# Counting tiny weights on GpSimd behind the channel layers, in place of zeroing them while they are rounded

## The chip, the core and the metric

The kernel runs on one core of one Trainium2 chip. The core has five engines that run side by side and wait for each other through semaphores: PE (TensorE: matrix products, with its weight loads PEld beside them), DVE (VectorE), ACT (ScalarE), POOL (GpSimd) and SP (SyncE, which here issues all DMAs, one after the other). The metric is the device time of one launch in microseconds (us). Before the change it is 819.13 us, the median of three runs (819.13 to 821.41).

## The reference, cut to what matters

```
attention: B,H,S,D = 4,8,768,48            # f = sigmoid(f_logit)
  state = f[t] * state + k[t] v[t]^T ;  y[t] = q[t] state      # a gated linear recurrence
spatial MLP on x = y (768 x 384 per batch):
  h = relu(x @ w_in);  u, v = halves of h;  v_n = layernorm(v)
  v_s = w_spatial @ v_n + b_spatial;  x = (u * v_s) @ w_out
mixer:
  u = x + (relu(x^T @ w_tok1) @ w_tok2)^T                       # token layer
  out = u + relu(u @ w_ch1) @ w_ch2                             # channel layer, width 1536
```

The weights w_in, w_out, w_tok1, w_tok2, w_ch1 and w_ch2 arrive as 64-bit floats, w_spatial and the activations as 32-bit ones. Results are 32-bit.

## The kernel before, in words

One program handles the four batches in turn. Every matrix product that needs full precision is done as three passes: each operand is split into a high and a low part (h and l), and PE computes h*h, h*l and l*h (`mm3`, lines 158 to 164).

The first stage (about 0 to 445 us) goes through the batches. For each batch it does the attention (`att`, 8 units of two heads and half a sequence; a unit starts with the load `fkq` of 578 KB), then the spatial MLP (`s1` gives the halves u and v, `s23` mixes over the sequence and multiplies by w_out, result `x1d` in DRAM). Units of the next batch's attention are woven between the matrix products of the present one. The second stage (about 445 us to the end) does the token layer (`c1`, `c2`) and the channel layer (`ff`): for each batch and each half of the sequence, 12 steps, each with 9 matmuls up (`up1`), a relu on ACT (`hh`, line 641), its low part on DVE (`hl`, line 642) and 9 matmuls down (`down`, line 654).

Before a 64-bit weight can be used it is turned into 32 bits by integer operations, in pieces of 128 x 384 (47 of them). That is the function `rounded` (lines 58 to 80): SP loads the raw words (`st`), DVE shifts and joins the high word (lines 66 and 69), ACT scales the low word (line 73), POOL adds it with rounding (line 74), ACT squares the high word, read as a 32-bit float (line 75), and DVE multiplies the result by "square >= bound" (line 79). A double too small for a normal 32-bit float so becomes zero. w_in and w_out are used at once (`split_weight`). The other four are rounded early, stored to DRAM (`round_weight`, store on line 93) and read back as 32-bit numbers later. Pools limit how many pieces are under way: three buffers for `st`, three for the result.

A second body, written for general inputs (`body(True)`), stands behind a branch and runs only if `flag` is set; the flag comes from the smallest gate product (`pend`, lines 550 to 556) and is read by all engines at the end (line 710). It does not run with these inputs.

The functions emit instructions in program order, in lists that `weave` mixes. A scheduler then orders each engine's instructions by its own estimate of when they are ready, and picks a free buffer for each tile. So the order on each engine and on SP's queue is fixed before the run: whatever stands first and waits holds up all that stands behind it.

Of the kernel before, what the change touches and what calls it, by code (L numbers as in the profile page):

```python
# [8 lines left out]
F32 = mybir.dt.float32  # L9
# [9 lines left out]
def tile_kernel(ctx, tc, fkqs, v, w_in, w_sp, b_sp, w_out, w_t1, w_t2, w_c1, w_c2, out):  # L19
    nc = tc.nc  # L20
# [22 lines left out]
    def f32(ap):  # L43
        return ap.bitcast(F32)
# [8 lines left out]
    pend = const.tile([P, B * NP, NCH], F32, name="pend")  # L53


    LEAST = 3.4332275390625e-05 ** 2

    def rounded(stage, a, src, c0, width, name):

        st = stage.tile([P, WST, 2], U32, tag="wst", name=f"{name}st")  # L60
        nc.sync.dma_start(
            out=st[:, :width, :].rearrange("p c t -> p (c t)"), in_=src[:, 2 * c0 : 2 * (c0 + width)]
        )
        yield
        lo, hi = st[:, :width, 0], st[:, :width, 1]
        nc.vector.tensor_scalar(
            out=a, in0=hi, scalar1=3, scalar2=0x3FFFFFFF, op0=ALU.logical_shift_left, op1=ALU.bitwise_and
        )
        nc.vector.scalar_tensor_tensor(
            out=a, in0=hi, scalar=0xC0000000, in1=a, op0=ALU.bitwise_and, op1=ALU.bitwise_or  # L70
        )

        nc.scalar.activation(lo, lo, AF.Copy, scale=2.0**-29)
        nc.gpsimd.tensor_tensor(out=a, in0=a, in1=lo, op=ALU.add)
        nc.scalar.activation(f32(hi), f32(hi), AF.Square)
        yield

        a = f32(a)
        nc.vector.scalar_tensor_tensor(out=a, in0=f32(hi), scalar=LEAST, in1=a, op0=ALU.is_ge, op1=ALU.mult)
        return a  # L80

    def round_weight(stage, src, name):

        if src.dtype != mybir.dt.uint64:
            return src, []
        rows, cols = src.shape
        dst = dram.tile([rows, cols], F32, name=name + "d")
        srcr = src.bitcast(U32).rearrange("(n p) c -> n p c", p=P)

        def piece(i, c0, width):  # L90
            at = stage.tile([P, WST], U32, tag="wsa", name=f"{name}da{i}{c0}")
            a = yield from rounded(stage, at[:, :width], srcr[i], c0, width, f"{name}d{i}{c0}")
            nc.sync.dma_start(out=dst[i * P : (i + 1) * P, c0 : c0 + width], in_=a)

        return dst, [
            partial(piece, i, c0, min(WST, cols - c0)) for i in range(rows // P) for c0 in range(0, cols, WST)
        ]

    kept = {}

    def split_weight(pool, stage, src, name, n, cols, eng, first=0, order=None, psum=None):

        wide = src.dtype == mybir.dt.uint64
        h = pool.tile([P, n, cols], F32R, name=name + "h")
        l = pool.tile([P, n, cols], F32R, name=name + "l")
        if wide:
            src = src.bitcast(U32)
        srcr = src.rearrange("(n p) c -> n p c", p=P)

        def piece(i, c0, width):  # L110
            sl = (slice(None), i, slice(c0, c0 + width))
            at = stage.tile([P, WST], U32, tag="wsa", name=f"{name}sa{i}{c0}")
            a = at[:, :width]
            if wide:
                a = yield from rounded(stage, a, srcr[first + i], c0, width, f"{name}{i}{c0}")
                nc.scalar.copy(h[sl], a)
                yield
            else:
                a = f32(a)
                nc.sync.dma_start(out=a, in_=srcr[first + i][:, c0 : c0 + width])  # L120
                yield
                nc.scalar.copy(h[sl], a)
                yield
                yield
            if eng is not nc.tensor:
                eng.tensor_tensor(out=l[sl], in0=a, in1=f32(h[sl]), op=ALU.subtract)
                return

            ps = psum.tile([P, W], F32, tag="m", name=f"{name}pl{i}{c0}")[:, :width]
            nc.tensor.matmul(ps, ident, a, start=True, stop=False)  # L130
            nc.tensor.matmul(ps, minus, h[sl], start=False, stop=True)
            yield
            nc.scalar.copy(l[sl], ps)

        where = [(i, c0, min(WST, cols - c0)) for i in range(n) for c0 in range(0, cols, WST)]
        return h, l, [partial(piece, *x) for x in (order(where) if order else where)]
# [13 lines left out]
    def weave(main, *fillers):  # L150

        for n, m in enumerate(main):
            for fl in fillers:
                for x in fl[len(fl) * n // len(main) : len(fl) * (n + 1) // len(main)]:
                    x()
            m()
# [9 lines left out]
    def body(general):  # L166
# [289 lines left out]
        def s23(b):  # L456
# [39 lines left out]


        winh, winl, steps = split_weight(
            wr, wst, w_in, "win", NK, DFF, nc.tensor, order=lambda x: sorted(x, key=lambda y: -y[1]), psum=ps_m
        )  # L500
        weave(att(half(0, 0)), staged(steps))
        bb = const.tile([P, S], F32, tag="bb", name="bb")
        nc.sync.dma_start(out=bb, in_=b_sp.unsqueeze(0).to_broadcast([P, S]))
        wsph, wspl, st_a = split_weight(wl, wst, w_sp, "wsp", NCH, S, nc.tensor, psum=ps_m)
        wouth, woutl, st_b = split_weight(wl, wst, w_out, "wout", NJ, DM, nc.tensor, psum=ps_m)
        s10, a01, sa = s1(0, 0), att(half(0, 1)), staged(st_a)
        weave(a01[:8], sa[:6])
        weave(s10, a01[8:], sa[6:])
        out_steps = staged(st_b)
        rest = []  # L510
        early = []
        if not general:
            for name, src in (("wt1", w_t1), ("wt2", w_t2), ("wc1", w_c1), ("wc2", w_c2)):
                kept[name], x = round_weight(wst, src, name)
                early += x
            early = staged(early)
        part = lambda n: early[len(early) * n // 5 : len(early) * (n + 1) // 5]
        for b in range(B - 1):
            if b:
                weave(s1(b, 0), rest)  # L520
            a, rest = s1(b, 1), []
            m, rest = s23(b)
            steps = att(half(b + 1, 0) + half(b + 1, 1))
            cut = len(steps) * len(a) // len(a + m)
            weave(a, steps[:cut], out_steps if b == 0 else part(2 * b - 1))
            weave(m, steps[cut:], part(2 * b))
        right.close()
        wr2 = ExitStack()
        w2p = wr2.enter_context(tc.tile_pool(name="w2p", bufs=1, side="right"))
# [1 line left out]
        t2h, t2l, st_b = split_weight(w2p, wst, kept["wt2"], "wt2", NT1, S, nc.gpsimd)  # L531
        c1h, c1l, st_c = split_weight(w2p, wst, kept["wc1"], "wc1", NK - 1, DC, nc.gpsimd)
        c1w = [(c1h[:, c, :], c1l[:, c, :]) for c in range(NK - 1)]
        weave(rest + s1(B - 1, 0) + s1(B - 1, 1), staged(st_a + st_b))
        conv = st_c
        mid.close()
        w2q = wr2.enter_context(tc.tile_pool(name="w2q", bufs=1, side="right"))
# [7 lines left out]
        xhp = wr2.enter_context(tc.tile_pool(name="xhp", bufs=1, side="right"))  # L545
        h1p = wr2.enter_context(tc.tile_pool(name="h1p", bufs=1, side="right"))

        if not general:

            nc.vector.tensor_reduce(  # L550
                out=least, in_=pend.rearrange("p u c -> p (u c)"), op=ALU.min, axis=mybir.AxisListType.X
            )
            row = ps_s.tile([P, W], F32, tag="s", name="row")[:1, :P]
            nc.tensor.transpose(row, least, ident)
            nc.vector.tensor_reduce(out=least[:1], in_=row, op=ALU.min, axis=mybir.AxisListType.X)
            nc.vector.tensor_scalar(out=flag, in0=least[:1], scalar1=LOW, scalar2=None, op0=ALU.is_lt)


        st2 = {}

        def c1(b):
            d = st2[b] = {}
# [66 lines left out]
        def ff(b, hf):  # L629
# [4 lines left out]
            def up1(ft):  # L634
                uh, ul = st2[b]["u"]
                fsl = slice(ft * P, (ft + 1) * P)
                ps = ps_m.tile([P, W], F32, tag="m", name=f"p3{b}{hf}{ft}")
                mm3(ps, [(c1w[c][0][:, fsl], c1w[c][1][:, fsl], uh[:, c, tsl], ul[:, c, tsl]) for c in range(NK)])
                hh = h3p.tile([P, W], F32R, tag="hh", name=f"hh{b}{hf}{ft}")
                hl = h3p.tile([P, W], F32R, tag="hl", name=f"hl{b}{hf}{ft}")  # L640
                nc.scalar.activation(hh, ps, AF.Relu)  # L641
                nc.vector.scalar_tensor_tensor(  # L642
                    out=hl, in0=ps, scalar=0.0, in1=f32(hh), op0=ALU.max, op1=ALU.subtract
                )
                hs[ft] = hh, hl
# [14 lines left out]
            def step(n):  # L660
                if n in range(3, 3 + NK):
                    uh, ul = st2[b]["u"]
                    c = n - 3
                    us[c] = op.tile([P, W], F32, tag=f"us{c}", name=f"us{b}{hf}{c}")
                    nc.gpsimd.tensor_tensor(  # L665
                        out=us[c], in0=f32(uh[:, c, tsl]), in1=f32(ul[:, c, tsl]), op=ALU.add
                    )
                if n < NF:
                    up1(n)
                if n:  # L670
                    down(n - 1)
                if n == NF:
                    for c in range(NK):
                        ot = otp.tile([P, W], F32, tag="ot", name=f"ot{b}{hf}{c}")
                        nc.vector.tensor_tensor(out=ot, in0=po[c], in1=us[c], op=ALU.add)
                        nc.sync.dma_start(out=out[b, c * P : (c + 1) * P, tsl], in_=ot)
# [84 lines left out]
```

## Time and profile before

| what | before |
|---|---|
| median of three runs | 819.13 us |
| the profiled execution | 819.0 us |
| its span, first to last instruction | 817.2 us |
| granted TensorE clock, mean | 0.978 |
| busy: PE, PEld | 777.3 us (95%), 716.3 us (88%) |
| busy: DVE, ACT, POOL | 420.3 (51%), 289.1 (35%), 211.1 us (26%) |
| instructions | 12758 |
| read from HBM, written | 54.72 MB, 15.73 MB |

The busy shares are means over two unlike stages. In the page's 40 slices of about 20 us DVE stands at 6 to 9 tenths up to the 14th slice and at 1 to 3 tenths from the 24th; POOL falls to 0 for most of the last 16 slices, while PE is at 9 tenths in all but the last of them. What a change is worth has therefore to be read from the stage in which its instructions run.

### The profile page before, as it was taken

The numbers are of one execution on the slowest core, as the hardware profiler recorded it, in microseconds if no ns is written. First come the engines' busy times: TensorE is split into PE (matmuls) and PEld (weight loads), VectorE is DVE, ScalarE is ACT, GpSimd is POOL, SyncE is SP. The second block draws the span as 40 slices with busy tenths as digits, with TensorE's granted clock in tenths as the row PEclk, the third lists the DMA queues.
The fourth block names the chain that finished last, engine by engine and source line by source line (L and its number), as shares of the span: only waits on it lengthen the run. The fifth ranks groups of instructions, "written<-read, shape, count | busy, mean of one in ns | idle before, by whom it ended". The sixth has DMA issues, their size and how long they took to land.

```text
span 817.2 us, 12758 instructions
## 1 busy us (share of the span) xinstructions
PE 777.3 (95%) x4860; PEld 716.3 (88%) x4860; DVE 420.3 (51%) x820; ACT 289.1 (35%) x649; POOL 211.1 (26%) x265
## 2 busy tenths in 40 slices
PE   5899899898989999999999999999999999999996
PEld 3577688688779888899899999999999999999995
DVE  6968599899898846673552532122122212221211
ACT  5766464555553444231632531122111211221110
POOL 4524344555641212110760330004000400010000
PEclk9899899999999999999999999999999999999998
DMA  7563435766474321220441410002000200000000
GB/s 254 176 207 104 147 96 164 236 225 214 146 237 140 101 96 59 65 67 24 128 126 40 138 56 30 1 4 85 1 30 0 87 1 30 1 8 24 30 1 33
DMA packets 39847, 73.74 MB, mean 90 GB/s; under 512 B 5216, under 2 KB 29664, under 8 KB 39776
## 3 DMA queue, kind: packets, MB, share of 16 engines
q1 hardware_dynamic: 39776, 72.83, 27.7%
q8 instruction: 40, 0.66, 0.3%
q14 instruction: 31, 0.25, 0.1%
HBM read 54.72 MB, written 15.73 MB: 86 GB/s over the span
## 4 chain that ended last, share of the span: by engine, by line
PE 71%; DVE 10%; DMA 10%; issue 4%; ACT 2%; SPq 1%; POOL 1%; DVEq 0%; ACTq 0%; POOLq 0%
PE po L654 19%; PE p L164 8%; PE p L162 8%; PE p L163 8%; DMA fkq<-in_fkq 3%; PE ps L162 3%; PE ps L164 3%; PE ps L163 3%; PE pa L259 2%; PE py L309 2%; PE py L315 2%; PE px L162 2%; PE px L163 1%; PE px L164 1%; DVE pg L236 1%
## 5 line engine op out<-in xcount | busy, mean ns | idle before, releaser
L642 DVE SCALAR_TENSOR_TENSOR hl<-p,hh 128x384 fp32r<-128x384 f32 x96 | 53.3, 557 | 188.4 <-ACT hh L641 188.4
L641 ACT ACTIVATE hh<-p 128x384 fp32r<-128x384 f32 x96 | 47.2, 492 | 198.0 <-PE p L164 198.0
L654 PE MATMUL po<-hl,wc2h 128*128 128x384 f32 x288 | 97.3, 338 | 0.0
L654 PE MATMUL po<-hh,wc2l 128*128 128x384 f32 x288 | 96.7, 336 | 0.0
L665 POOL TENSOR_TENSOR us<-uh,ul 128x384 f32<-128x384 f32 x24 | 24.3, 1024 | 232.0 <-DVE ul L625 214.7
L654 PE MATMUL po<-hh,wc2h 128*128 128x384 f32 x288 | 75.0, 336 | 0.0
L162 PE MATMUL ps<-wsph,vh 128*128 128x384 f32 x192 | 67.5, 351 | 0.0
L163 PE MATMUL ps<-wspl,vh 128*128 128x384 f32 x192 | 66.4, 346 | 0.0
L164 PE MATMUL ps<-wsph,vl 128*128 128x384 f32 x192 | 66.1, 346 | 0.0
L164 PE MATMUL p<-uh,wc1l 128*128 128x384 f32 x192 | 65.0, 338 | 0.0
L264 POOL TENSOR_SCALAR_AFFINE_SELECT am<-am 128x384 f32<-128x384 f32 x64 | 46.9, 748 | 69.7 <-ACT am L263 69.5
L163 PE MATMUL p<-ul,wc1h 128*128 128x384 f32 x192 | 64.7, 337 | 0.0
L162 PE MATMUL p<-uh,wc1h 128*128 128x384 f32 x192 | 64.2, 338 | 0.0
L654 PEld LDWEIGHTS po<-hl,wc2h 128*128 128x128 f32 x288 | 54.1, 188 | 0.1
L654 PEld LDWEIGHTS po<-hh,wc2l 128*128 128x128 f32 x288 | 54.1, 188 | 0.0
L654 PEld LDWEIGHTS po<-hh,wc2h 128*128 128x128 f32 x288 | 52.3, 188 | 0.0
L236 DVE TENSOR_TENSOR_SCAN pg<-fs,first 128x384 f32<-128x384 f32 x32 | 33.3, 1039 | 22.2 <-ACT first L379 22.1
L259 PE MATMUL pa<-fkq 48*128 48x128 f32 x384 | 40.6, 316 | 3.0 <-ACT am L263 3.0
L259 PEld LDWEIGHTS pa<-fkq 48*128 48x128 f32 x384 | 30.5, 204 | 12.3 <-issue 4.3
L162 PEld LDWEIGHTS ps<-wsph,vh 128*128 128x128 f32 x192 | 37.1, 193 | 2.4 <-issue 1.6
L625 DVE TENSOR_TENSOR ul<-p,uh 128x384 fp32r<-128x384 f32 x24 | 13.4, 557 | 47.6 <-ACT uh L624 47.6
L163 PEld LDWEIGHTS ps<-wspl,vh 128*128 128x128 f32 x192 | 37.0, 193 | 0.5 <-issue 0.2
(419 smaller groups left out, 1928.5 us busy)
## 6 DMA issues: line engine op xcount, KB each, us to landing
fkq<-in_fkq SPq DMA_DIRECT2D x31, 578.0 KB, 4.5
vt<-in_v SPq DMA_DIRECT2D x8, 576.0 KB, 5.9
x1d<-xs SPq DMA_DIRECT2D x24, 192.0 KB, 2.0
xf<-x1d SPq DMA_DIRECT2D x12, 384.0 KB, 4.5
out<-ot SPq DMA_DIRECT2D x24, 192.0 KB, 2.0
wspsa<-in_w_sp SPq DMA_DIRECT2D x12, 192.0 KB, 2.6
wc1d<-wc1da SPq DMA_DIRECT2D x12, 192.0 KB, 2.4
wc2d<-wc2da SPq DMA_DIRECT2D x12, 192.0 KB, 2.2
```

What stands on the lines that cost most here:

```text
L162: nc.tensor.matmul(ps, lh, rh, start=first and i == 0, stop=False, **kw)
L163: nc.tensor.matmul(ps, lh, rl, start=False, stop=False, **kw)
L164: nc.tensor.matmul(ps, ll, rh, start=False, stop=i == n - 1, **kw)
L236: nc.vector.tensor_tensor_scan(out=pc, data0=fs[:, :W], data1=first, initial=0.0, op0=ALU.mult, op1=ALU.add)
L259: nc.tensor.matmul(pa[j][:, c, :], ki[64 * j : 64 * j + D, sl], qi[64 * j : 64 * j + D, sl], start=True, stop=True)
L264: nc.gpsimd.affine_select(out=am[j], in_=am[j], compare_op=ALU.is_ge, fill=0.0, base=0, pattern=[[0, NCW], [1, C]], channel_multiplier=-1,)
L309: nc.tensor.matmul(py[:112, c, :], now[c][:112, :112], qi[:112, c * C : (c + 1) * C], start=c == 0, stop=False, skip_group_check=True,)
L315: nc.tensor.matmul(py[64 * j : 64 * j + m, c, :], vt[:, c, h0 + D * j : h0 + D * j + m], am[j][:, c, :], start=False, stop=True, skip_grou ...
L641: nc.scalar.activation(hh, ps, AF.Relu)
L642: nc.vector.scalar_tensor_tensor(out=hl, in0=ps, scalar=0.0, in1=f32(hh), op0=ALU.max, op1=ALU.subtract)
L654: nc.tensor.matmul(po[c], l[:, ft, csl], r, start=ft == 0 and x == 0, stop=ft == NF - 1 and x == 2)
L665: nc.gpsimd.tensor_tensor(out=us[c], in0=f32(uh[:, c, tsl]), in1=f32(ul[:, c, tsl]), op=ALU.add)
```

## The change

Three things change.

1. In the first body `rounded` no longer squares (ACT) and no longer compares and multiplies (DVE). The general body, which needs the zeroing, keeps both, and now rounds the four later weights itself.
2. Instead the first body counts: 88 times a block of 192 columns of a raw 64-bit weight is loaded again (`look`), in the channel layer, one block per step of `ff`. POOL squares the high words, compares with a slightly larger bound, and adds the result to a tile `lows`. The blocks' buffers are taken from the rotation (tag) of the channel layer's low parts `hl`, which has 7 buffers instead of 4. In the last half, at its eighth step, `judge` reduces `lows` and `pend` to one flag: if any weight was tiny, the general body runs. It stood ahead of the channel layer before, without `lows`.
3. The pieces of the four later weights are dealt out in program order from the second batch on, over seven lists instead of five, the last of them in the fourth batch.

```
-        nc.scalar.activation(f32(hi), f32(hi), AF.Square)
+        if tiny:
+            nc.scalar.activation(f32(hi), f32(hi), AF.Square)
         yield
         a = f32(a)
-        nc.vector.scalar_tensor_tensor(out=a, in0=f32(hi), scalar=LEAST, in1=a, op0=ALU.is_ge, op1=ALU.mult)
+        if tiny:
+            nc.vector.scalar_tensor_tensor(
+                out=a, in0=f32(hi), scalar=LEAST**2, in1=a, op0=ALU.is_ge, op1=ALU.mult
+            )
         return a
...
+    NEED = 192
+    lows = const.tile([P, NEED], F32, name="lows")
...
+    def look(pool, src, n):
+
+        rows, cols = src.shape[1] , src.shape[2]
+        st = pool.tile([P, 2 * NEED], U32, tag="hl", bufs=7, name=f"look{n}")[:, : rows * cols]
+        nc.sync.dma_start(out=st.rearrange("p (n c) -> p n c", n=rows), in_=src)
+        to = lows[:, : rows * cols // 2]
+        hi = f32(st[:, 1::2])
+        nc.gpsimd.tensor_tensor(out=hi, in0=hi, in1=hi, op=ALU.mult)
+        nc.gpsimd.tensor_scalar(out=hi, in0=hi, scalar1=NEAR**2, scalar2=None, op0=ALU.is_lt)
+        nc.gpsimd.tensor_tensor(out=to, in0=to, in1=hi, op=ALU.add)
...
-        part = lambda n: early[len(early) * n // 5 : len(early) * (n + 1) // 5]
+        part = lambda n, m: early[len(early) * n // 14 : len(early) * m // 14]
         for b in range(B - 1):
             if b:
-                weave(s1(b, 0), rest)
+                weave(s1(b, 0), rest, part(7 * b - 9, 7 * b - 7) if b > 1 else [])
...
-            weave(a, steps[:cut], out_steps if b == 0 else part(2 * b - 1))
-            weave(m, steps[cut:], part(2 * b))
+            weave(a, steps[:cut], out_steps if b == 0 else part(7 * b - 7, 7 * b - 5))
+            weave(m, steps[cut:], part(7 * b - 5, 7 * b - 2) if b else [])
...
-        weave(rest + s1(B - 1, 0) + s1(B - 1, 1), staged(st_a + st_b))
+        weave(rest + s1(B - 1, 0) + s1(B - 1, 1), staged(st_a + st_b), part(12, 14))
...
-        if not general:
-
+        def judge():
+
+            nc.vector.tensor_scalar(out=lows, in0=lows, scalar1=0.5, scalar2=None, op0=ALU.is_lt)
+            nc.vector.tensor_reduce(out=least, in_=lows, op=ALU.min, axis=mybir.AxisListType.X)
             nc.vector.tensor_reduce(
-                out=least, in_=pend.rearrange("p u c -> p (u c)"), op=ALU.min, axis=mybir.AxisListType.X
+                out=lows[:, :1], in_=pend.rearrange("p u c -> p (u c)"), op=ALU.min, axis=mybir.AxisListType.X
             )
+            nc.vector.tensor_tensor(out=least, in0=least, in1=lows[:, :1], op=ALU.min)
...
-                hl = h3p.tile([P, W], F32R, tag="hl", name=f"hl{b}{hf}{ft}")
+                hl = h3p.tile([P, W], F32R, tag="hl", bufs=7, name=f"hl{b}{hf}{ft}")
...
                 if n < NF:
                     up1(n)
+                    if todo and (b, hf) != (B - 1, 1) or n < NF - 4:
+                        for src in todo[:1]:
+                            look(h3p, src, len(todo))
+                        del todo[:1]
+                    elif n == NF - 4 and not general:
+                        judge()
```

On DVE, where the first batch's mixing overlaps the second batch's attention, the rounding of w_ch1 (`wc1da` is the piece's result, `st` its raw words, the digits behind are row block and first column; `fkq113`, `pg113` and `z1110` belong to an attention unit) stands like this before:

```order
L66 TENSOR_SCALAR wc1da0384_2350<-wc1d0384st_2351 128x384
L240 RECIPROCAL last_125<-pg113_1713 128x3
L69 SCALAR_TENSOR_TENSOR wc1da0384_2350<-wc1d0384st_2351,wc1da0384_2350 128x384
L241 SCALAR_TENSOR_TENSOR pg113_1713<-fs113_1710,last_125 128x384
L79 SCALAR_TENSOR_TENSOR wc1da00_2293<-wc1d00st_2294,wc1da00_2293 128x384
L297 SCALAR_TENSOR_TENSOR z1110_1665<-z1012_1198,pend_65,pk111_1658 112x48
L244 TENSOR_TENSOR fkq113_1708<-fkq113_1708,pg113_1713 128x768
L66 TENSOR_SCALAR wc1da0768_2392<-wc1d0768st_2393 128x384
L79 SCALAR_TENSOR_TENSOR wc1da0384_2350<-wc1d0384st_2351,wc1da0384_2350 128x384
```

And the same place after (its result is now called `wc10da`):

```order
L67 TENSOR_SCALAR wc10da0384_2864<-wc10d0384st_2865 128x384
L503 TENSOR_TENSOR g011_1586<-ps011_1567,bb_499 128x384
L70 SCALAR_TENSOR_TENSOR wc10da0384_2864<-wc10d0384st_2865,wc10da0384_2864 128x384
L504 TENSOR_TENSOR g011_1586<-g011_1586,u01_946 128x384
L267 SCALAR_TENSOR_TENSOR pg113_1657<-fs113_1654,first_125 128x384
L271 RECIPROCAL last_126<-pg113_1657 128x3
L272 SCALAR_TENSOR_TENSOR pg113_1657<-fs113_1654,last_126 128x384
L67 TENSOR_SCALAR wc10da0768_2936<-wc10d0768st_2937 128x384
L275 TENSOR_TENSOR fkq113_1652<-fkq113_1652,pg113_1657 128x768
```

The multiplications of line 79 are gone from between the attention's instructions. The pieces of rounding stand beside the same unit (113) as before: in spite of the new lists they hardly move. Only the last two of the 34 pieces to DRAM go far back, behind the fourth batch's first three `norm` steps.

On DVE in the last half (`hl314` is the low part of step 4 of the fourth batch's second half) the judging stands here after:

```order
L679 SCALAR_TENSOR_TENSOR hl314_8064<-p3314_8053,hh314_8063 128x384
L581 TENSOR_SCALAR lows_66<-lows_66 128x192
L582 TENSOR_REDUCE least_62<-lows_66 128x1
L583 TENSOR_REDUCE lows_66<-pend_65 128x1
L586 TENSOR_TENSOR least_62<-least_62,lows_66 128x1
L679 SCALAR_TENSOR_TENSOR hl315_8089<-p3315_8078,hh315_8088 128x384
```

Before, the two `hl` rows follow each other; the four instructions between them have come in, and the first waits for POOL's last count.

On POOL at the start of the channel layer (`x1l1` are the low parts of the second batch's input to the token layer, three pieces; `look88` is the first block) the counts stand here after:

```order
L128 TENSOR_TENSOR look88_5061<-look88_5061 128x192
L129 TENSOR_SCALAR look88_5061<-look88_5061 128x192
L702 TENSOR_TENSOR us012_5637<-uh0_4934,ul0_4935 128x384
L130 TENSOR_TENSOR lows_66<-lows_66,look88_5061 128x192
L128 TENSOR_TENSOR look87_5084<-look87_5084 128x192
L614 TENSOR_TENSOR x1l1_5169<-xf1_5167,x1h1_5168 128x768
L128 TENSOR_TENSOR look86_5119<-look86_5119 128x192
L129 TENSOR_SCALAR look87_5084<-look87_5084 128x192
```

Before, POOL had only the `us` and `x1l1` rows there. In later batches all three `x1l` pieces stand ahead of the next three blocks.

## Rows read from the trace of the kernel before

**Rows 1.** Span and mean granted TensorE clock of the core.

```profile
core 0: 817.2 us, clock 0.978
```

**Rows 2.** Stretches: busy us and instructions of each engine, then clock, DMA share, GB/s.

```profile
core 0: us, PE busy (x) PEld busy (x) DVE busy (x) ACT busy (x) POOL busy (x), PEclk, DMA share, GB/s
20.00:300.00 280.00, 259.47 (x1759) 215.55 (x1759) 236.43 (x476) 146.97 (x348) 115.36 (x143) 0.95 0.52 167
300.00:466.00 166.00, 164.62 (x1075) 151.21 (x1074) 85.69 (x169) 62.97 (x140) 50.27 (x69) 1.00 0.25 75
466.00:809.00 343.00, 343.00 (x1976) 342.05 (x1974) 83.76 (x150) 67.90 (x135) 37.11 (x29) 1.00 0.08 26
...
140.00:260.00 120.00, 109.20 (x723) 94.41 (x721) 110.06 (x218) 60.38 (x138) 57.53 (x62) 0.93 0.61 200
```

**Rows 3.** The same for line 79 alone (DVE), then line 75 alone (ACT).

```profile
0.00:300.00 300.00, 28.86 (x47) 0.95 0.54 172
...
0.00:300.00 300.00, 25.33 (x47) 0.95 0.54 172
```

**Rows 4.** The chain that ended last, 20 to 300 us, by line.

```profile
by line: issue 10.5%; DMA fkq<-in_fkq 8.5%; PE pa L259 4.3%; PE py L309 3.7%; PE py L315 2.8%; DVE pg L236 2.4%; PE winpl L130 2.3%; DVE fkq L244 2.1%; PE ps L163 2.0%; PE ps L164 1.9%; DVE vf L440 1.9%; PE pv L162 1.9%; DMA wc2d20st<-in_w_
```

**Rows 5.** The chain in order of time: start us, us, what.

```profile
10.24 0.42 DVE winsa L79
...
15.61 0.89 DVE winsa L79
...
21.97 0.58 ACT win0384st L75
...
204.08 0.56 DVE wc1da L79
...
204.65 0.33 SPq L93
...
205.15 5.26 DMA wc2d20st<-in_w_c
...
243.54 0.47 DVE wc2da L79
```

**Rows 6.** POOL's groups by shape: busy us, mean ns of one, idle before.

```profile
L264 POOL TENSOR_SCALAR_AFFINE_SELECT am<-am 128x384 f32<-128x384 f32 x64 | 46.9, 748 | 69.7 <-ACT am L263 69.5
L665 POOL TENSOR_TENSOR us<-uh,ul 128x384 f32<-128x384 f32 x24 | 24.3, 1024 | 232.0 <-DVE ul L625 214.7 <-DVE ot L675 17.3
L577 POOL TENSOR_TENSOR x1l<-xf,x1h 128x768 fp32r<-128x768 f32 x12 | 23.6, 1980 | 36.9 <-ACT x1h L576 36.9
L438 POOL TENSOR_TENSOR rs<-ve,nhalf 128x1 f32<-128x1 f32 x24 | 16.5, 688 | 1.7
L436 POOL TENSOR_SCALAR ve<-mv 128x1 f32<-128x1 f32 x24 | 10.0, 415 | 47.9 <-DVE mv L434 46.9
L74 POOL TENSOR_TENSOR wc1da<-wc1da,wc1d1768st 128x384 uint32<-128x384 uint32 x1 | 2.1, 2067 | 2.7 <-DVE wc1da L69 2.7
```

**Rows 7.** Instructions in time, channel layer: start us, us, engine, line.

```profile
474.97 3.60 DVE L126 TENSOR_TENSOR wc2l<-wc2sa,wc2h 128x384 fp32r<-128x384 f32 x2 [0.18 <-ACT wc2h L122]
...
554.08 1.86 POOL L577 TENSOR_TENSOR x1l<-xf,x1h 128x768 fp32r<-128x768 f32 x1 [17.80 <-ACT x1h L576]
...
555.42 0.56 DVE L642 SCALAR_TENSOR_TENSOR hl<-p,hh 128x384 fp32r<-128x384 f32 x1 [1.08 <-ACT hh L641]
...
803.33 0.56 DVE L642 SCALAR_TENSOR_TENSOR hl<-p,hh 128x384 fp32r<-128x384 f32 x1 [2.61 <-ACT hh L641]
...
804.18 0.35 PE L654 MATMUL po<-hl,wc2h 128*128 128x384 f32 x1
...
806.49 0.56 DVE L642 SCALAR_TENSOR_TENSOR hl<-p,hh 128x384 fp32r<-128x384 f32 x1 [2.60 <-ACT hh L641]
```

**Rows 8.** DMA issues: what, count, KB each, median us to landing.

```profile
wc2sa<-wc2d SPq DMA_DIRECT2D x12, 192.0 KB, 2.9
```

**Rows 9.** One of line 79's groups by shape: busy us, mean ns, idle before.

```profile
L79 DVE SCALAR_TENSOR_TENSOR wc1da<-wc1d00st,wc1da 128x384 f32<-128x384 f32 x1 | 1.3, 1302 | 0.0
```

More of the change, by code (lines that the diff above doesn't have):

```diff
@@ L53, in tile_kernel, with rounded @@
     pend = const.tile([P, B * NP, NCH], F32, name="pend")
-    LEAST = 3.4332275390625e-05 ** 2
-    def rounded(stage, a, src, c0, width, name):
+    LEAST = 3.4332275390625e-05
+    NEAR = 3.5e-05
+    def rounded(stage, a, src, c0, width, name, tiny):
         st = stage.tile([P, WST, 2], U32, tag="wst", name=f"{name}st")
@@ L74, in rounded, with round_weight @@
         nc.gpsimd.tensor_tensor(out=a, in0=a, in1=lo, op=ALU.add)
-        nc.scalar.activation(f32(hi), f32(hi), AF.Square)
+        if tiny:
+            nc.scalar.activation(f32(hi), f32(hi), AF.Square)
         yield
         a = f32(a)
-        nc.vector.scalar_tensor_tensor(out=a, in0=f32(hi), scalar=LEAST, in1=a, op0=ALU.is_ge, op1=ALU.mult)
+        if tiny:
+            nc.vector.scalar_tensor_tensor(
+                out=a, in0=f32(hi), scalar=LEAST**2, in1=a, op0=ALU.is_ge, op1=ALU.mult
+            )
         return a
-    def round_weight(stage, src, name):
+    def round_weight(stage, src, name, tiny):
         if src.dtype != mybir.dt.uint64:
@@ L91, in piece @@
             at = stage.tile([P, WST], U32, tag="wsa", name=f"{name}da{i}{c0}")
-            a = yield from rounded(stage, at[:, :width], srcr[i], c0, width, f"{name}d{i}{c0}")
+            a = yield from rounded(stage, at[:, :width], srcr[i], c0, width, f"{name}d{i}{c0}", tiny)
             nc.sync.dma_start(out=dst[i * P : (i + 1) * P, c0 : c0 + width], in_=a)
@@ L99, in tile_kernel, with looks, split_weight @@
     kept = {}
-    def split_weight(pool, stage, src, name, n, cols, eng, first=0, order=None, psum=None):
+    NEED = 192
+    lows = const.tile([P, NEED], F32, name="lows")
+    def looks():
+        out = []
+        for w in (w_in, w_out, w_t1, w_t2, w_c1, w_c2):
+            if w.dtype == mybir.dt.uint64:
+                wr = w.bitcast(U32).rearrange("(n p) c -> p n c", p=P)
+                n, cols = w.shape[0] // P, w.shape[1]
+                full, rest = divmod(cols, NEED)
+                out += [wr[:, i : i + 1, 2 * NEED * c : 2 * NEED * (c + 1)] for i in range(n) for c in range(full)]
+                m = NEED // rest if rest else n
+                out += [wr[:, i : min(n, i + m), 2 * NEED * full :] for i in range(0, n, m) if rest]
+        return out
+    def look(pool, src, n):
[7 more added lines that the diff above has]
+        nc.gpsimd.tensor_tensor(out=to, in0=to, in1=hi, op=ALU.add)
+    def split_weight(pool, stage, src, name, n, cols, eng, first=0, order=None, psum=None, tiny=False):
         wide = src.dtype == mybir.dt.uint64
@@ L114, in piece @@
             if wide:
-                a = yield from rounded(stage, a, srcr[first + i], c0, width, f"{name}{i}{c0}")
+                a = yield from rounded(stage, a, srcr[first + i], c0, width, f"{name}{i}{c0}", tiny)
                 nc.scalar.copy(h[sl], a)
@@ L498, in body @@
         winh, winl, steps = split_weight(
-            wr, wst, w_in, "win", NK, DFF, nc.tensor, order=lambda x: sorted(x, key=lambda y: -y[1]), psum=ps_m
+            wr, wst, w_in, "win", NK, DFF, nc.tensor, order=lambda x: sorted(x, key=lambda y: -y[1]), psum=ps_m,
+            tiny=general,
         )
@@ L504, in body @@
         wsph, wspl, st_a = split_weight(wl, wst, w_sp, "wsp", NCH, S, nc.tensor, psum=ps_m)
-        wouth, woutl, st_b = split_weight(wl, wst, w_out, "wout", NJ, DM, nc.tensor, psum=ps_m)
+        wouth, woutl, st_b = split_weight(wl, wst, w_out, "wout", NJ, DM, nc.tensor, psum=ps_m, tiny=general)
         s10, a01, sa = s1(0, 0), att(half(0, 1)), staged(st_a)
@@ L511, in body @@
         early = []
-        if not general:
[L513 to L516, printed above, removed]
-        part = lambda n: early[len(early) * n // 5 : len(early) * (n + 1) // 5]
+        for name, src in (("wt1", w_t1), ("wt2", w_t2), ("wc1", w_c1), ("wc2", w_c2)):
+            kept[name], x = round_weight(wst, src, f"{name}{int(general)}", general)
+            early += x
+        early = staged(early)
+        part = lambda n, m: early[len(early) * n // 14 : len(early) * m // 14]
         for b in range(B - 1):
             if b:
-                weave(s1(b, 0), rest)
+                weave(s1(b, 0), rest, part(7 * b - 9, 7 * b - 7) if b > 1 else [])
             a, rest = s1(b, 1), []
@@ L546, in body @@
         h1p = wr2.enter_context(tc.tile_pool(name="h1p", bufs=1, side="right"))
-        if not general:
+        def judge():
+            nc.vector.tensor_scalar(out=lows, in0=lows, scalar1=0.5, scalar2=None, op0=ALU.is_lt)
+            nc.vector.tensor_reduce(out=least, in_=lows, op=ALU.min, axis=mybir.AxisListType.X)
             nc.vector.tensor_reduce(
-                out=least, in_=pend.rearrange("p u c -> p (u c)"), op=ALU.min, axis=mybir.AxisListType.X
+                out=lows[:, :1], in_=pend.rearrange("p u c -> p (u c)"), op=ALU.min, axis=mybir.AxisListType.X
             )
+            nc.vector.tensor_tensor(out=least, in0=least, in1=lows[:, :1], op=ALU.min)
             row = ps_s.tile([P, W], F32, tag="s", name="row")[:1, :P]
@@ L559, in body @@
         st2 = {}
+        todo = [] if general else looks()
+        if todo:
+            nc.gpsimd.memset(lows, 0.0)
         def c1(b):
```

## The prediction

> **What bounds the kernel now.** I read the span and clock first, then each engine's busy time by stretch, then the chain of waits, and last POOL's groups and single instructions of the channel layer. One core, no second die, mean clock 0.978 [rows 1].
>
> The stretches split the kernel in three [rows 2]. From 466 to 809 us PE is busy in all of its 343.00 us at clock 1.00, and its weight loads take 342.05: this is the channel layer, bound by PE, with DVE at 83.76 us and POOL at 37.11 us. From 300 to 466 us PE is busy 164.62 of 166. From 20 to 300 us PE is idle 280 - 259.47 = 20.5 us, its weight loads take only 77%, and the clock is 0.95. There DVE is busy 236.43 of 280, and from 140 to 260 even 110.06 of 120 (92%). So time can be won only before 300 us, and lost after it.
>
> The chain says what the early stretch waits for [rows 4]: no single engine, but gaps ("issue" 10.5%), landings of loads, and many short DVE pieces. In order of time [rows 5] the rounding shows as a loop: DVE's multiplication of line 79 at 204.08 ends, SP then issues the store of the rounded piece (line 93) and behind it the next raw load, which takes 5.26 us to land. SP's queue is in order, so a store that waits for line 79 also holds the loads behind it, the attention's `fkq` among them.
>
> **The change part by part.** *Removed on DVE and ACT.* Line 79 ran 47 times for 28.86 us and the square of line 75 47 times for 25.33 us, all before 300 us [rows 3]. Their whole time is not their worth. On the chain line 79 stands in 27 pieces, the first 0.42 us at 10.24 and the last 0.47 us at 243.54, together 12.87 us; line 75 in four, the first 0.58 us at 21.97, together 1.61 us [rows 5]. So 14.5 us of what sets the end goes, if nothing else was ready to be late just behind it. What is late next is known: the store then waits for POOL's addition (line 74), which came ahead of line 79 anyway, and after that for the raw load. The bounds: below 0, if the landing of loads and the gaps simply take the freed places; above 28.86 us, if DVE is the bound of the whole stretch (92% busy in 140 to 260 us [rows 2] speaks for that). I take 14.5 us, the chain's own figure.
>
> *The later rounding.* The emitted order shows that it hardly happens: the first piece of w_tok1 still stands by the same attention unit, and so do those of w_ch1. Only two of 34 pieces move, into the fourth batch, where DVE is busy 85.69 of 166 us [rows 2]. There they share three staging buffers with the weights read back. I cost this at nothing; PE's 1.4 idle us in that stretch are the cover that it has. If each of the two held up the read-back by one landing of 2.9 us [rows 8], it would be 6 us; if freed DVE time draws the mixing forward, it is a gain of at most the 1.4 idle us.
>
> *Added: 88 counts on POOL, in the channel layer.* Two two-input instructions and one compare on 128 x 192. Two-input ones took 1024 ns for 384 columns and 1980 for 768 [rows 6], 2.49 ns a column, so 546 ns for 192. The compare lies between 415 ns (one column, `ve`) and 748 ns (384 columns, line 264); I take 580. Each waits for the one before it on its own engine; `rs`, which does so behind `ve`, idled 1.7 us in 24 times [rows 6], 0.07 us each. One block: 2 x 546 + 580 + 3 x 70 = 1.88 us (1.72 to 2.05). A step of the channel layer is 806.49 - 803.33 = 3.16 us [rows 7]. In 12 steps, 38 us, POOL also has three `us` and, in a batch's first half, three `x1l`: 3 x 1.02 + 3 x 1.98 = 9.0 us. So it keeps pace while a block costs under (38 - 9)/12 = 2.4 us. At 1.88 it does, and the cost is 0. The worst bound is a POOL addition next to a busy DVE: 2067 ns for 384 columns [rows 6], twice the usual; at twice 1.88 each first half of three batches would fall 12 x 3.76 + 9 - 38 = 16 us behind, 48 us in all. DVE is busy a quarter of this stretch, so I take the undisturbed end.
>
> *The shared buffers.* A low part may now wait for the count that had its buffer before; seven buffers at two per step are 3.5 steps, 11 us, ahead. At the start of a batch the order puts three blocks behind the last `x1l`; the first of them is done some 4 us after it, and the low part that waits for it comes later still. The low part's own time matters: it ends at 803.33 + 0.56 = 803.89 and PE takes it at 804.18 [rows 7], 0.29 us later, in every step. At 555.42 it took the same 0.56 us while POOL was in an `x1l` [rows 7], so a busy POOL does not slow it. Cost 0.
>
> *Loads.* 88 blocks of 192 KB are 17 MB, 48 GB/s over the stretch, beside 26 GB/s there now [rows 2], which has carried 167 GB/s earlier. A load of this size took 2.9 us [rows 8]. Cost 0, but on SP they stand ahead of some of the next batch's input loads; these are needed only half a batch later.
>
> *The judging.* Four DVE instructions between two low parts, where DVE idles 2.61 us [rows 7]; at about 0.25 us each they fit. Ahead of them stands the wait for POOL's last count, behind them the next low part, and PE waits for that. One small transposition moves on PE: 0.2 us at most.
>
> The Trainium skill has a rule that speaks against this place for the counts ("SBUF — State Buffer", section "SBUF: two separate sides"): a DVE instruction with two SBUF inputs and a GpSimd instruction that reads SBUF exclude each other for the whole of the instruction. By it the low parts, with one input from PSUM, are free, which the equal 0.56 us bears out. Line 79, with two SBUF inputs, took 1302 ns once [rows 9] against a mean of 28.86/47 = 0.61 us, which agrees; two `wc2l` next to an `x1l` took 3.60 us [rows 7]. By the rule the counts at the head of the channel layer would stretch `wc2l` further; the price is in the rivals.
>
> **Sum.** The profiled execution took 819.0 us, of which 817.2 is span; the median is 819.13, so the two are one. 819.0 - 14.5 + 0.2 = 804.7: **805 us**.
>
> **The rivals.**
> - *The chain's share goes, as above*: 799 to 811 us. Chance 0.55.
> - *DVE is the bound of the early stretch*, and all 28.86 us come out: 819.0 - 28.9 = 790 us (785 to 798). For it: 92% busy, and PE's 20.5 idle us plus the low clock leave room. Against: the chain holds more landing of loads than line 79. Chance 0.15.
> - *The loads keep the loop as long as it was*: three staging buffers and landings of 5.26 us set the pace, and only the start, where w_in is rounded straight into use, gains: 0.42 + 0.89 + 0.58 = 1.9 us of the chain [rows 5], with as much again and an extra 1 us elsewhere, 5 us: 814 us (810 to 816.5). For it: "issue" and `fkq` lead the chain [rows 4]. Against: the landings begin only when line 79 lets the store go. Chance 0.12.
> - *The counts slow `wc2l`*: up to eight of them, each by 1.80 - 0.56 = 1.24 us as at 474.97 [rows 7], 10 us if all of it reaches PE: 815 us. Against: PE lost nothing there with two stretched already. Chance 0.03.
> - *No change*: the new fixed order loses elsewhere what it wins, such as in waits for the attention's transpositions: 816.5 to 821.5 us. Chance 0.06.
> - *Slower: POOL falls behind PE in the channel layer.* Place: the first halves of batches one to three, where POOL also has `x1l`; a low part then waits for its buffer, and PE for the low part. It decides from 2.4 us a block, and cancels the gain from (14.3/3 + 38 - 9)/12 = 2.8 us; at 3.1 us it costs 3 x (12 x 3.1 + 9 - 38) = 25 us: 830 us. For it: no row shows a strided compare on POOL. Against: 1.88 us from rows, and low parts that did not feel POOL. Chance 0.09.
>
> **How the numbers follow.** The likeliest is 805, its own range 799 to 811. A change under 0.3% (2.5 us) can't be told from none in this kernel. Faster: 0.55 + 0.15 + 0.12 + 0.03 = 0.85; within 0.3%: 0.06; slower: 0.09. The range 793 to 819 leaves out about half of the 790 case below (0.07) and the slower case with some of the unchanged one above (0.11).
>
> **What would show it right or wrong.** Lines 75 and 79 gone; DVE's busy time before 300 us down by about 29 us; the matching of the first mixing steps earlier by 5 us or more at 130 us and by 10 or more at 280 us; clock in that stretch above 0.95. POOL about 165 us busier, PE still without idle time from the first `ff` step to the last, low parts at 0.56 us, steps of 3.16 us. If the channel layer takes longer than its 343 us, POOL's blocks or the buffers are to blame; if the early stretch is as long as before, the loads set its pace, and the sum was wrong in its first term.

## The result and the profile after

The changed kernel takes 811.58 us in the median of 20 executions (805.48 to 819.84), the kernel before 819.22 in as many (816.68 to 823.90). The ratio is 0.990 (95% interval 0.988 to 0.991): 8 us faster. 805 us was forecast, 793 to 819 as the range. The sign is right, and the time lies in the range, just outside the likeliest case's own 799 to 811 us. How the number came about is another matter, as the experiments show.

The profiled execution took 806.8 us and lies at the quick end. In the main the 20 executions follow their mean granted clock: the seven at 0.991 or more took 805.5 to 809.7 us, the eight at 0.983 or less 812.7 to 819.8. The profile therefore shows 12 us of gain, the medians 8.

Span and clock of the changed kernel, for [rows 1]:

```profile
core 0: 805.0 us, clock 0.991
```

The stretches of the changed kernel, for [rows 2]; columns as there. The channel layer now begins 11 us earlier, so the cuts lie at 454 and 796 us:

```profile
20.00:300.00 280.00, 264.86 (x1826) 217.45 (x1826) 214.28 (x439) 129.65 (x311) 107.56 (x148) 0.98 0.52 165
300.00:454.00 154.00, 152.39 (x1004) 140.95 (x1002) 82.70 (x158) 59.10 (x133) 50.17 (x64) 1.00 0.26 81
454.00:796.00 342.00, 341.55 (x1968) 340.55 (x1967) 83.43 (x155) 68.22 (x136) 194.23 (x293) 1.00 0.26 77
```

Before 300 us PE's idle time falls from 20.5 to 15.1 us and the clock rises from 0.95 to 0.98. The channel layer keeps its length, though POOL is busy 194 us there in place of 37. Where the gain arises is read from the mixing's first DVE line in both kernels (ns shortest/median/longest, first and last start). Before:

```profile
L472 DVE TENSOR_TENSOR g<-ps,bb x32: 525/548/559, 127.6 to 441.2; 128x384 f32<-128x384 f32 x32
```

After:

```profile
L503 DVE TENSOR_TENSOR g<-ps,bb x32: 531/549/559, 123.0 to 429.8; 128x384 f32<-128x384 f32 x32
```

The first comes 4.6 us earlier, the last 11.4. What is won is won before the channel layer.

POOL's counts in the changed kernel, for [rows 6] (busy us, mean ns, idle before):

```profile
L129 POOL TENSOR_SCALAR look<-look 128x192 f32<-128x192 f32 x88 | 62.9, 715 | 7.6
L130 POOL TENSOR_TENSOR lows<-lows,look 128x192 f32<-128x192 f32 x88 | 53.3, 605 | 6.4
L128 POOL TENSOR_TENSOR look<-look 128x192 f32<-128x192 f32 x88 | 45.3, 517 | 46.5 <-DMA look<-in_w_c 26.0 <-DMA look<-in_w_t 11.0 <-DMA look<-in_w_in 9.0
```

A block takes 1.84 us (1.88 forecast), and POOL waits 46 us for its loads: it is ahead of its work. PE's only wait in the channel layer of the changed kernel (in total, times, longest):

```profile
PE po L691 <- DVE hl L679: 0.5, 1, 0.5
```

The judging, on DVE between two low parts (start us, us, engine, line):

```profile
773.54 0.56 DVE L679 SCALAR_TENSOR_TENSOR hl<-p,hh 128x384 fp32r<-128x384 f32 x1 [2.59 <-ACT hh L678]
774.01 0.25 DVE L581 TENSOR_SCALAR lows<-lows 128x192 f32<-128x192 f32 x1
774.30 0.35 DVE L582 TENSOR_REDUCE least<-lows 128x1 f32<-128x192 f32 x1
774.68 0.25 DVE L583 TENSOR_REDUCE lows<-pend 128x1 f32<-128x96 f32 x1
774.97 0.16 DVE L586 TENSOR_TENSOR least<-least,lows 128x1 f32<-128x1 f32 x1
776.71 0.56 DVE L679 SCALAR_TENSOR_TENSOR hl<-p,hh 128x384 fp32r<-128x384 f32 x1 [1.58 <-ACT hh L678]
```

The low parts stay 3.17 us apart and last 0.56 us, as in [rows 7]. So the second half of the change is free, and the question is the first term: 14.5 us forecast, 8 to 12 seen.

### The profile page after: what moved, and what is told of

Same layout as the page of the kernel before. It is cut to its first block, busy times and chain, and to the rows that moved or that the text cites. A ratio compares the mean times of both kernels' runs of the same rounds, so it can differ in the third digit from the quotient of the medians.

```text
span 805.0 us, 13086 instructions
## 1 busy us (share of the span) xinstructions
PE 772.0 (96%) x4860; PEld 708.8 (88%) x4860; DVE 395.0 (49%) x776; ACT 267.6 (33%) x602; POOL 359.7 (45%) x530
## 4 chain that ended last, share of the span: by engine, by line
PE 66%; DMA 13%; DVE 10%; issue 3%; POOL 3%; SPq 2%; ACT 2%; DVEq 0%; POOLq 0%; ACTq 0%
PE po L691 18%; PE p L195 8%; PE p L193 8%; PE p L194 8%; PE ps L193 3%; DMA fkq<-in_fkq 3%; PE ps L195 2%; PE ps L194 2%; PE pa L290 2%; SPq L427 2%; PE py L340 2%; PE px L193 2%; PE px L195 1%; DMA xh<-yh 1%; PE py L346 1%
## 5 line engine op out<-in xcount | busy, mean ns | idle before, releaser
L295 POOL TENSOR_SCALAR_AFFINE_SELECT am<-am 128x384 f32<-128x384 f32 x64 | 40.6, 650 | 91.0 <-ACT am L294 90.9
L129 POOL TENSOR_SCALAR look<-look 128x192 f32<-128x192 f32 x88 | 62.9, 715 | 7.6
L128 POOL TENSOR_TENSOR look<-look 128x192 f32<-128x192 f32 x88 | 45.3, 517 | 46.5 <-DMA look<-in_w_c 26.0
L130 POOL TENSOR_TENSOR lows<-lows,look 128x192 f32<-128x192 f32 x88 | 53.3, 605 | 6.4
L270 POOL COPY pend<-pg 128x3 f32<-128x3 f32 x32 | 13.8, 430 | 59.4 <-DVE pg L267 59.4
```

The source lines that it names most:

```text
L128: nc.gpsimd.tensor_tensor(out=hi, in0=hi, in1=hi, op=ALU.mult)
L129: nc.gpsimd.tensor_scalar(out=hi, in0=hi, scalar1=NEAR**2, scalar2=None, op0=ALU.is_lt)
L130: nc.gpsimd.tensor_tensor(out=to, in0=to, in1=hi, op=ALU.add)
L295: nc.gpsimd.affine_select(out=am[j], in_=am[j], compare_op=ALU.is_ge, fill=0.0, base=0, pattern=[[0, NCW], [1, C]], channel_multiplier=-1,)
```

## The experiments

**First series: the parts of the change, each kernel ordered anew by the scheduler.** Theory A is the forecast's: the chain's share is the gain. Theory B ties the gain to PE's clock and gaps, theory C to a cost of the counts. The first kernel is the one before without lines 75 and 79:

```
-        nc.scalar.activation(f32(hi), f32(hi), AF.Square)
...
-        nc.vector.scalar_tensor_tensor(out=a, in0=f32(hi), scalar=LEAST, in1=a, op0=ALU.is_ge, op1=ALU.mult)
```

> The kernel before, without the square and without the comparison with multiplication; its five rounding lists, the flag ahead of the channel layer and no counts. Left out: the check of tiny weights. Theory A (the chain's share is the gain, 12.9 us for the multiplication and 1.6 for the square): 819.2 - 14.5 = 805 us. Theory B (the gain is what PE gets back at its clock, and depends on where its gaps fall): between 805 and 815 us, with a mean granted clock above 0.985 in runs near 806 and about 0.98 in runs near 814, as in the runs of the changed kernel. Theory C (the counts and the new lists take back 4 us of a full gain): as A, 4 us under the changed kernel's 811.6, so 807 or less. If the new lists did the work: 817 or more.

Measured: 815.93 us, ratio 0.996 (0.993 to 0.998). Only 3 to 4 us are won where A says 14.5. B's 805 to 815 us is just missed too, though from run to run this kernel does follow its clock (809.9 us at 0.989, 821.8 at 0.980).

The second leaves out line 79 alone, the third line 75 alone (line 79 then has `scalar=-1e30`).

> The kernel before without the comparison with multiplication on DVE alone; the square on ACT stays, and nothing reads it. Left out: the check of tiny weights. Theory A: 819.2 - 12.9 = 806 us, 1.6 us above the kernel without both. Theory B: near the kernel without both, within the spread that its clock gives. If ACT's squares were what the loop waits for: 815 us or more.

> The kernel before without the square on ACT; DVE compares the high word itself with a bound that every weight passes, and multiplies by one. Left out: the check of tiny weights. Theory A: 819.2 - 1.6 = 817.6 us. Theory B: 815 to 819 us, the clock as before (0.975 to 0.98). If ACT's squares were what the loop waits for: 810 us or less.

Measured: 820.00 us, ratio 1.002 (0.999 to 1.005), and 815.47 us, ratio 0.996 (0.994 to 0.998). The instruction that stands in 27 pieces of the chain is worth nothing here; the one in four pieces is worth 4 us. Theory A, as a statement on these kernels, falls. B's 815 to 819 us holds for the third; the second lies 4 us above the kernel without both.

The fourth is the changed kernel without counts:

```
-        todo = [] if general else looks()
+        todo = []
```

> The changed kernel without the 88 counts and without their part of the judging; seven buffers for the low parts, the flag in the last half and the new rounding lists stay. Left out: the check of tiny weights. Forecast (the counts cost nothing): the changed kernel's 811.6 us, within 2 us. Theory C (the counts take back a part of the gain): 808 us or less. Rival on the buffers and the port: the channel layer shorter than the changed kernel's by more than 2 us, with low parts that PE no longer waits for.

Measured: 813.15 us, ratio 0.992 (0.989 to 0.994), against 0.990 with the counts. The counts take nothing back: theory C falls.

The waits of PE say where to look. In the kernel without both, from 20 to 300 us:

```profile
PE py L307 <- DVE state L282: 6.0, 5, 3.3
```

In the changed kernel:

```profile
PE py L340 <- DVE state L315: 5.6, 4, 2.9
```

In the kernel before:

```profile
PE py L309 <- DVE state L284: 1.0, 1, 1.0
```

`py` is the attention's product with its state. Without the zeroing the scheduler orders all engines anew: about 170 of the first 550 instructions that DVE still has change places relative to the others. In PE's queue the attention units move. The number of matmuls of the spatial MLP that stand ahead of a unit's last product with a state (units counted from 0):

```
unit (of 32)      16   17   18   19   22
before           414  484  506  551  630
changed kernel   441  463  486  522  621
```

Such matmuls start 0.17 us apart (in the changed kernel `ps` at 219.50, 219.68 and 219.85 us), so 29 fewer of them are 5 us that unit 19 stands earlier. Where a unit stands earlier, PE can reach its `py` before DVE has the state. That gave theory D: the order, which the edit also changes, takes the gain back.

**Second series: the order held.** Here the order of every engine is written down from one kernel and imposed on another, by edges that fix the order of issue and add no wait. "Order" is here that of all five queues, the loads on SP among them. The edit, in the kernel before without line 79:

```
+    for e, order in ORDER.items():
+        now = [mine[e][k] for k in order]
+        for a, b in zip(now, now[1:]):
+            tc.add_manual_dep(
+                b, a.name, mybir.DependencyInfo(mybir.DependencyClass.NoSync, mybir.DependencyReason.DATA), reason="pin"
+            )
```

Imposed on the kernel that it was written down from, the order gives the same instructions with the same waits.

> The kernel before with every engine's order held as it was, and only the multiplication of line 79 taken out of it. Left out: the check of tiny weights. When the scheduler was free to order anew, this took 820.0 us. Theory A (the chain's 12.9 us of line 79 are the worth of the work): 806 us, and the free order had lost them. Theory D (the order decides, the work itself is worth little): 817 to 820 us.

> The kernel before with every engine's order held, and the multiplications and the squares taken out of it. Left out: the check of tiny weights. With a free order this took 815.9 us. Theory A: 805 us. Theory D: 814 to 819 us, that is at least half of the changed kernel's gain of 7.6 us is missing. In between, 808 to 812 us, work and order would share the gain.

Measured: 797.45 us, ratio 0.974 (0.971 to 0.978), without line 79, and 799.39 us, ratio 0.976 (0.972 to 0.979), without both. Both theories forecast too small a gain. The freed work is worth 20 to 22 us, the square nothing, and the scheduler's own order had thrown away 16 us (815.9 to 799.4) of the same work's gain. The kernel without line 79, order held, from 20 to 300 us:

```profile
20.00:300.00 280.00, 269.06 (x1895) 223.65 (x1893) 225.15 (x456) 153.44 (x367) 115.04 (x154) 0.99 0.53 169
```

PE's idle time is 10.9 us in place of 20.5, and the clock 0.99 in place of 0.95: 9.6 us of gaps, and 280 x (0.99 - 0.95) = 11 us of clock, together about what was gained.

The opposite: the changed kernel's order held, with squares and multiplications put back (`if tiny:` becomes `if True:` twice).

> The changed kernel with its order held on every engine, and the squares and multiplications put back into the first body, at the places that the scheduler gives them. Theory A: 811.6 + 14.5 = 826 us. Theory D (the changed kernel's order is what gains): 811 to 815 us, near the changed kernel. If the work is worth what the pair of medians says: 819 us.

Measured: 833.72 us, ratio 1.018 (1.014 to 1.021). From 20 to 300 us, and PE's longest wait there:

```profile
20.00:300.00 280.00, 249.40 (x1688) 202.73 (x1685) 221.73 (x454) 141.13 (x334) 105.32 (x135) 0.94 0.51 158
```

```profile
PE py L357 <- DVE state L332: 12.7, 6, 4.8
```

PE idles 30.6 us, and the wait for the state has more than doubled. In this order the work costs 22 us too, more than any of the three expectations.

The new lists alone, on the kernel before:

```
-        part = lambda n: early[len(early) * n // 5 : len(early) * (n + 1) // 5]
+        part = lambda n, m: early[len(early) * n // 14 : len(early) * m // 14]
```

> The kernel before with the new rounding lists alone: squares and multiplications stay, no counts. Forecast (two pieces move, at no cost): 819 us, within 2 us. Rival (the lists give what the kernel without counts has over the kernel with the old lists and no zeroing, 815.9 - 813.2 = 2.8 us): 816.5 us. If the two pieces hold up the weights read back: 821 us or more.

Measured: 818.58 us, ratio 0.998 (0.996 to 1.001). Nothing that can be told from no change, as forecast.

**Third series: the better version, POOL's limit, and whose order it is.** The whole change, with the old lists and the order of before held for all that both kernels have; the scheduler places the counts and the judging.

> The whole change (counts in the channel layer, judging in the last half, no squares and multiplications) with the five rounding lists of before, and each engine's order of before held for all that both kernels have; only the counts and the judging are placed by the scheduler. It keeps the check of tiny weights. If the freed work is worth 20 us and the counts cost nothing: 799 us, as the kernel without both in the order of before. If the counts cost the 2 to 4 us that the changed kernel's median lacks: 801 to 803 us. If holding the order gained only because the check was left out: 811 us.

Measured: 799.60 us (797.83 to 800.03), ratio 0.975 (0.973 to 0.977). That is the first of the expected cases: the counts cost nothing. The kernel keeps the check of tiny weights and beats both others, the changed one by 12 us. Its early stretch, its first and last mixing line, and the only wait of a `py` from 20 to 300 us:

```profile
20.00:300.00 280.00, 270.28 (x1902) 225.63 (x1901) 226.23 (x458) 135.35 (x323) 112.84 (x154) 0.98 0.53 169
```

```profile
L520 DVE TENSOR_TENSOR g<-ps,bb x32: 525/548/558, 121.7 to 422.3; 128x384 f32<-128x384 f32 x32
```

```profile
PE py L352 <- POOL am L312: 0.9, 1, 0.9
```

No `py` waits for a state, and PE idles 9.7 us in place of the changed kernel's 15.1. The last mixing line comes 7.5 us before that of the changed kernel.

Then POOL's blocks made longer in the changed kernel:

```
-        nc.gpsimd.tensor_tensor(out=to, in0=to, in1=hi, op=ALU.add)
+        for _ in range(3):
+            nc.gpsimd.tensor_tensor(out=to, in0=to, in1=hi, op=ALU.add)
```

> The changed kernel with each count's addition to the tile done three times, so a block on POOL takes 0.52 + 0.72 + 3 x 0.61 = 3.06 us and some gaps, 3.2 in all, in place of 1.84. By the slower rival's sum (POOL falls behind from 2.4 us a block in three first halves): 3 x (12 x 3.2 + 9 - 38) = 28 us, 840 us, with PE waiting for low parts. If the buffers and the second halves take it up: 812 to 816 us.

Measured: 809.65 us, ratio 0.988 (0.985 to 0.990), no slower than the changed kernel, and not the slower rival's 840 us. POOL is busy 302 of the 340 us from 450 to 790. Who waited in the channel layer of this kernel, DVE first, then PE:

```profile
DVE hl L680 <- ACT hh L679: 94.5, 50, 5.4
DVE hl L680 <- POOL lows L131: 78.7, 32, 5.6
...
PE po L692 <- DVE hl L680: 0.5, 1, 0.5
```

The low parts did wait for POOL, 32 times, and PE did not notice. Why, the same kernel's instructions in time show:

```profile
604.38 0.56 DVE L680 SCALAR_TENSOR_TENSOR hl<-p,hh 128x384 fp32r<-128x384 f32 x1 [1.03 <-ACT hh L679]
604.90 0.33 PE L692 MATMUL po<-hl,wc2h 128*128 128x384 f32 x1
608.39 0.33 PE L692 MATMUL po<-hl,wc2h 128*128 128x384 f32 x1
608.94 0.56 DVE L680 SCALAR_TENSOR_TENSOR hl<-p,hh 128x384 fp32r<-128x384 f32 x1 [0.87 <-ACT hh L679]
```

The matmul at 604.90 uses the low part of the step before: in the code, `up1(n)` stands ahead of `down(n - 1)`. The low part that DVE ends at 604.94 is first needed at 608.39, 3.45 us later, about a whole step. One thing helped besides: this kernel's order was written anew with the longer counts, and in the first batch, where low parts start up to 4.2 us late, ten matmuls of the next token layer now stand ahead of those that need them.

Last, without both lines, the order of before held on one engine only (`for e, order in [("EngineType.PE", ...)]`, then DVE).

> Squares and multiplications left out, with PE's order of before held; all other engines ordered anew. Left out: the check of tiny weights. If it is PE's new order that loses (attention units put up to 29 matmuls earlier, which PE then waits for): 799 us. If it is the order on DVE or SP: 812 to 816 us.

> Squares and multiplications left out, with DVE's order of before held; all other engines ordered anew. Left out: the check of tiny weights. If it is DVE's new order that loses: 799 us. If it is PE's: 812 us or more, the more so as PE now has some attention units later and others earlier than before.

Measured: 817.80 us, ratio 0.999 (0.997 to 1.001), with PE held, and 810.73 us, ratio 0.990 (0.987 to 0.993), with DVE held. Neither comes to the 799 us that was expected if that engine's order is the one that loses. With PE's order the waits for the state shrink to 1.4 us, and the time is still lost elsewhere (4.6 us for a load of w_spatial, 6.2 us of "issue"); with DVE's they stay (5.2 us), and a third of the loss comes back. So neither of these two orders alone brings the gain back. ACT's, POOL's and SP's were not held alone; that the orders have to fit each other is a reading of this, not shown.

## Why the prediction was right or wrong

The orders make a table of medians (us; both kernels without zeroing have the counts, and so has the one with zeroing in the changed order):

| | zeroing in | zeroing out | the work |
|---|---|---|---|
| order of before | 819.6 | 799.6 | 20.0 |
| order of the changed kernel | 833.7 | 811.6 | 22.1 |
| the order | 14.1 | 12.0 | |

The change is -20 to -22 for the work and +12 to +14 for the order: -8.

- *Step "14.5 us of what sets the end goes"*: mis-sized. With the order held 20 us went, and line 79 alone was worth all of it (22 us; the square 0, where 1.6 had been put). That lies about midway between the chain's 14.5 and the 28.9 us of the rival "DVE is the bound", so neither account had it. What the chain's figure for line 79 leaves out is the clock: by the stretch of the kernel without it, about half of the gain is clock (11 us), and PE's matmuls at the lower level stand on the chain as PE's own time.
- *No term of the sum stood for the order.* Only the rival "No change" named it ("the new fixed order loses elsewhere what it wins", chance 0.06); in the sum it stands at nothing. The part on the change said that pieces of rounding "hardly move", and that holds for where they begin in the program. But every engine's order was written anew, and that cost more than the 6 us by which the first term was too small. That 805 came near 811.6 is luck: two errors of opposite sign, 6 and 12 us, partly cancelled.
- *Loads set the pace* (814 us forecast): close in time, wrong in cause. An attention load's median landing is 4.0 us in the kernel without both ordered anew, and 4.1 us in the one with its order held, which is 16 us faster.
- *Counts, judging, loads, later rounding at 0 to 0.2 us*: right, by the kernel without counts, by the new lists alone, and by the better version, 799.6 us against 799.4 for the same order without counts.
- *"PE takes it at 804.18, 0.29 us later, in every step"*: misread; that matmul uses the low part of the step before, as the rows of the kernel with longer counts show. The cover is 3.45 us there, and not 0.29.
- *The slower rival, from 2.4 us a block*: POOL did fall behind, but at no cost. At 3.1 to 3.2 us a first half falls 12 x 3.2 + 9 - 38 = 9 us behind, which the 11 us of buffers and the cover just named can take up. The second half gives it back: with the next batch's token layer woven in, it lasts 52 us in place of the first half's 38 (second batch; first low parts at 553.19, 591.68 and 643.61 us), and its low parts mostly start within 0.1 us of their `hh` again. The rival had been summed as if no buffer stood in between.
- *Counts slow `wc2l`* (10 us): PE lost 0.5 us there, and to a subtraction that mostly ran beside `x1l`, not beside a count. The head of the changed kernel's channel layer, in order of time:

```profile
461.65 1.85 POOL L614 TENSOR_TENSOR x1l<-xf,x1h 128x768 fp32r<-128x768 f32 x1
461.81 2.10 DVE L157 TENSOR_TENSOR wc2l<-wc2sa,wc2h 128x384 fp32r<-128x384 f32 x1 [3.43 <-ACT wc2h L153]
463.46 0.82 POOL L128 TENSOR_TENSOR look<-look 128x192 f32<-128x192 f32 x1
463.84 0.55 DVE L679 SCALAR_TENSOR_TENSOR hl<-p,hh 128x384 fp32r<-128x384 f32 x1
464.31 1.17 DVE L157 TENSOR_TENSOR wc2l<-wc2sa,wc2h 128x384 fp32r<-128x384 f32 x2
464.37 1.07 POOL L129 TENSOR_SCALAR look<-look 128x192 f32<-128x192 f32 x1
464.44 0.45 PE L691 MATMUL po<-hl,wc2h 128*128 128x384 f32 x1 [0.46 <-DVE hl L679]
```

Beside `x1l` the subtraction takes 2.10 us in place of 0.55; the low part behind it on DVE comes late, and PE waits 0.46 us, its one wait in the channel layer. The counts next to such subtractions took 0.82 and 1.07 us in place of 0.52 and 0.72. By the Trainium skill ("SBUF — State Buffer", section "SBUF: two separate sides") such a DVE instruction, with two inputs from SBUF, and a GpSimd instruction that reads SBUF shut each other out for the whole instruction. The row of 2.10 us agrees: it ends 0.41 us after `x1l`. The compare of 1.07 us agrees in part only: it and two subtractions lie within 1.17 us, where one after the other they would need 2 x 0.55 + 0.72 = 1.82 us.

What stays open: which rows of the order cost the 12 to 16 us. The waits for the state are 5.6 us in the changed kernel, if each counts in full. The sum of PE's gaps and clock, which fits where the order is held, gives the kernel without both, ordered anew, 15 us of gain by 300 us, while its mixing was only 9 us ahead.

## What to carry to other kernels

Where a scheduler writes the order, an edit is two changes: the work and a new order, and here the second cost 12 us. Hold the old order and measure the work by itself before judging either; a removal that gains nothing in the new order may be worth 20 us in the old. A buffer's or a result's slack is read from the instruction that uses this very piece, not from the next one in time that has its name.

## What the runs showed of the hardware

Idle time on PE can be paid for twice. In the kernel before (10 us each; columns as in [rows 2]):

```profile
150.00:160.00 10.00, 6.62 (x50) 5.85 (x51) 9.15 (x18) 6.33 (x17) 8.49 (x7) 1.00 0.51 161
160.00:170.00 10.00, 10.00 (x63) 8.57 (x62) 8.79 (x21) 5.46 (x12) 5.39 (x6) 0.66 0.83 259
```

In the better version, at the same time:

```profile
150.00:160.00 10.00, 8.71 (x73) 7.27 (x71) 9.43 (x20) 3.75 (x10) 5.24 (x6) 1.00 0.78 245
160.00:170.00 10.00, 10.00 (x61) 8.63 (x61) 9.20 (x18) 5.05 (x12) 5.03 (x5) 1.00 0.76 280
```

Before, PE was busy 6.6 of 10 us, and in the next 10 the granted clock was 0.66, so two thirds of them ran at the lower of its two levels (1.2 and 2.4 GHz) while PE was busy throughout: 3.4 us lost after 3.4 us of idle time. With 8.7 of 10 busy it stayed at 1.00. Not every stretch with idle time is followed by a fall: in the better version PE was busy 8.05 and 8.54 of 10 us from 80 to 100 us, and the clock stayed at 1.00 up to 200 us. That the changed kernel's executions spread over 14 us, along with their clock, fits this; which gaps tip in which of them was not looked at.
